# One block's second layer moved to the end part of a three-stage transformer kernel, with its activations parked in DRAM

## The chip, the core and the metric

The kernel runs on one core of one Trainium2 chip. The metric is the device time of one launch in microseconds (us), lower is better. The engines are named as the profile names them: PE (TensorE matmuls), PEld (weight loads), DVE (VectorE), ACT (ScalarE), POOL (GpSimd), SP (the queue from which most DMAs are issued).

## What is computed

Three stages follow each other: a masked attention, a gated layer pair with an RMS norm ahead of it, and a second layer pair with a leaky activation.

```python
# 4 batches, 8 heads, 576 positions, head size 64; heads 0-3 a window of 32, heads 4-7 every 4th of 128
scores = np.where(masks, scale * q @ k.T, -1e9)
x = softmax(scores) @ v                      # -> (2304, 512)
xn = x / sqrt(mean(x * x) + 1e-6) * rms_g
y = (silu(xn @ w_gate) * (xn @ w_val)) @ w_out      # 512 -> 1536 -> 512
h = y @ w_in                                        # 512 -> 2048
out = (max(h, 0) + alpha * min(h, 0)) @ w_out2      # 2048 -> 512
```

Inputs and the output are float32. The kernel splits each operand into two float16 halves (high and low) and adds three products (high by high, high by low, low by high) for each matrix product.

## The kernel before

The 2304 tokens are seven blocks: blocks 0, 1 and 5 have 256 tokens, blocks 2, 3, 4 and 6 have 384. In this text "A j" is the first layer pair of block j (`mm1`, `mm2`), 12 steps c of 128 hidden columns, and "B j" is the second one (`mm3`, `mm4`), 16 steps. In step c of B j, `mm3` makes 12 matmuls (4 slices of the model width by 3 half products) that stream the block's tokens, ACT and DVE form the activation (lines 984 and 985), ACT and POOL split it into halves, and two steps later `mm4` adds it into the block's sum with 3 matmuls of 512 columns for each 128 tokens. `y_out` (lines 957 to 966 of before) ends A j: it scales the 128-token tiles of y, splits them into halves in a tile `yhl`, and transposes them by a DMA from SP into `xy[j % 3]`, one of three buffers that hold a block's x and later its y.

The order of the phases is written out by hand: A0, A1, A2, B0, B1, B2, A3, then the first four steps of A4, B3, the rest of A4, A5, A6. Blocks 4, 5 and 6 have no B phase. Their second layer runs in an end part over pairs of 128-token tiles (list `tiles`, four pairs): `mm3_t` makes the same products as `mm3`, two steps c at a time, and `mm4_t` makes the last product in a form with 7 block products in place of 8, each a 128x256 product in three half products. So a pair needs 192 matmuls of 256 columns in `mm3_t` and 8 x 21 = 168 of 256 columns in `mm4_t`; the pair's sums are put together in `out_t` (m1o at line 1120, yo at lines 1123 to 1127). The weights of the end part's last product are made up in `remake`, during A6.

The attention runs beside the layers. It is cut into 156 steps, and `take` hands out steps in each slot (one slot is one step c of a phase): it looks at the x of which block is due when, and paces the steps evenly to that, with a planner's clock that counts 1.95 for 128 tokens in an A slot and 1.3 in a B slot. In A2 the credit is multiplied by `PACE`, 0.7. Most of the attention is in groups of up to 128 queries: a split into halves (ACT lines 539 to 542, DVE 548 to 553), a DMA transpose `qkT<-qkhl` (line 563, one for each group), scores, exponentials (line 589), a second DMA transpose `pT<-phl`, the product with v, and for half of the groups the norm. The tiles `qkhl` and `qkT` have one buffer each.

The weights are loaded, unpacked on DVE (lines 231 to 233) and split on ACT, DVE and POOL (lines 404 to 409) beside the first phases: those of the first pair in A0, those of the second one at the end of A2 and in B0. All decoded weights together fill 68 of 70 slots of the tile `wb`; slots of the first pair's weights come free as A6 uses them for the last time.

A tile scheduler with a timeline of its own sets the order of the instructions on each engine within the priorities that the code gives; attention steps have a higher priority.

Of the kernel before, what the change touches and what calls it, by code (L numbers as in the profile page):

```python
# [29 lines left out]
def kernel(  # L30
# [14 lines left out]
    nc = tc.nc  # L45
# [901 lines left out]
    def y_out(j):  # L947
# [6 lines left out]
        for n in range(nt):  # L954
            y = wk.tile([128, 2, DM], F16, tag="hl2", bufs=2, name="yhl")
            hl.append(y)
            nc.scalar.activation(y.rearrange("p a d -> p (a d)").bitcast(F32), acc[n], ACTF.Square, accum_out=ss[:, n:n + 1])
            nc.vector.tensor_scalar(ss[:, n:n + 1], ss[:, n:n + 1], 2.0 ** -100, None, ALU.max)
            rcn = rc[:, n:n + 1]
            if j >= NTJ:  # L960
                i = tiles.index((j, n))
                rcn = rct[:, i:i + 1]
            root_scale(ss[:, n:n + 1], sg[:, n:n + 1], rcn, 2.0 ** -62)
            nc.scalar.activation(y[:, 0, :], acc[n], ACTF.Copy, scale=sg[:, n:n + 1])
            nc.vector.scalar_tensor_tensor(y[:, 1, :], acc[n], sg[:, n:n + 1], y[:, 0, :], ALU.mult, ALU.subtract)
# [52 lines left out]

    NTJ = 4
    NP = C2 // 2  # L1020

    tiles = [(4, 0), (4, 1), (5, 0), (5, 1), (4, 2), (6, 2), (6, 0), (6, 1)]
    assert sorted(tiles) == [(j, n) for j in range(NTJ, NJ) for n in range(ncols(j) // 128)]
    NT = len(tiles) // 2
# [30 lines left out]
    def weight(cp, m, l):  # L1055
# [3 lines left out]
        return ts[cp][l][:, w]  # L1059

    def mm3_t(t, cp):
        tl = tail["tl"]
        ps = tail["ps3"].tile([128, 2, 256], F32, tag="p3", name="p3")
        (j0, n0), (j1, n1) = tiles[2 * t:2 * t + 2]
        if (j0, n0 + 1) == (j1, n1):
            parts = [(0, 256, xy[j0 % NXY][:, :, :, n0 * 128:n0 * 128 + 256])]
# [198 lines left out]
    for s in slots:  # L1265
        kind, j, c = s
        for f in take(dur(s) * (PACE if (kind, j) == ("A", 2) else 1.0)):
            f()
# [9 lines left out]
        if kind == "A" and j < 3:  # L1278
# [30 lines left out]
    for n in range(len(order) + 1):  # L1309
        if n < len(order):  # L1310
# [50 lines left out]
```

## Time and profile before

| | |
|---|---|
| median of 3 runs | 956.49 us (955.83 to 957.1) |
| the profiled execution's own time | 959.12 us |
| its span, first to last instruction | 956.9 us |
| busy: PE / DVE / ACT / POOL | 906.7 / 666.4 / 548.2 / 321.2 us |
| A2 ends and B0 begins (first activation of line 984) | 294.3 us |
| first output of B0, B1, B2 (line 1002) | 346.4, 391.1, 454.9 us |
| end of A3 (line 957) | 529.6 us |
| end of A5, and first matmul of the end part | 724.6 and 790.3 us |

The profiled execution is one run; its time is 2.6 us above the median of the three timed ones. A span is counted from the first to the last instruction. A busy PE means that matmuls were under way, not that they follow each other at the highest rate.

### The profile page before, as it was taken

What the parts mean: (1) busy time and instruction counts of PE and PEld (TensorE: products, weight loads), DVE (VectorE), ACT (ScalarE), POOL (GpSimd) and SP (SyncE); (2) the same over time, 40 slices, a digit from 0 to 9 for tenths busy, and PEclk for the clock granted to TensorE, in tenths of its full rate; (3) what the DMA queues carried; (4) which work ended last, traced back from release to release, by engine and by line L of the source; (5) the groups of instructions that cost most, each with busy time, mean ns of one, the idle gap of its engine ahead of it and who ended that gap; (6) DMA issues with size and microseconds to landing.
All of it is one profiled execution on the core that took longest, in us unless ns stands there. A gap on an engine that the chain in (4) does not pass through costs nothing.

```text
span 956.9 us, 18827 instructions
## 1 busy us (share of the span) xinstructions
PE 906.7 (95%) x6760; PEld 619.6 (65%) x6760; DVE 666.4 (70%) x1602; ACT 548.2 (57%) x1537; POOL 321.2 (34%) x324
## 2 busy tenths in 40 slices
PE   6568899999998999999999999999999999999997
PEld 4556676775556666555555555555775558889986
DVE  4999997998787766665766775334545837777674
ACT  3436587766799886766756776444534324344342
POOL 2222441131354544423332233333252622322221
PEclk9778999999999999999999999999999999999998
DMA  9992346545324555544554654232301001000000
GB/s 255 315 357 89 120 131 188 143 146 149 81 51 99 106 101 94 106 85 95 117 93 82 114 97 71 59 76 42 54 15 23 1 1 35 1 24 23 2 24 23
DMA packets 191613, 88.14 MB, mean 92 GB/s; under 512 B 176800, under 2 KB 180384, under 8 KB 191520
## 3 DMA queue, kind: packets, MB, share of 16 engines
q1 hardware_dynamic: 189504, 83.27, 37.9%
q10 hardware_dynamic: 2016, 3.67, 1.2%
q8 instruction: 53, 0.87, 0.4%
q14 instruction: 40, 0.33, 0.1%
HBM read 55.32 MB, written 6.55 MB: 65 GB/s over the span
## 4 chain that ended last, share of the span: by engine, by line
PE 74%; DVE 10%; DMA 6%; ACT 4%; issue 2%; SPq 2%; POOL 1%; DVEq 0%; ACTq 0%; POOLq 0%
PE psw L97 34%; PE acc L97 22%; PE p L97 16%; DMA wb<-in_moe_w_out_dram 2%; DVE wb L232 2%; DVE wb L233 2%; ACT wb L404 2%; DVE wb L231 1%; DVE wb L409 1%; SPq L212 1%; SPq L629 1%; DMA wb<-in_moe_w_val_dram 1%; DMA wb<-in_moe_w_gate_dram 1%; DMA wb<-in_q_dram 1%; PE psw L639 1%
## 5 line engine op out<-in xcount | busy, mean ns | idle before, releaser
L97 PEld LDWEIGHTS <-wb 128*128 128x128 f16 (+1 forms) x4866 | 452.3, 98 | 196.5 <-DVE wb L233 18.9
L97 PE MATMUL psw<-xyall,wb 128*128 128x384 f16 (+1 forms) x2784 | 425.0, 303 | 2.1 <-DVE sqo L284 1.2
L97 PE MATMUL acc<-wb,hlall 128*128 128x512 f16 x822 | 197.1, 379 | 1.9 <-ACT hlall L924 1.1
L97 PEld LDWEIGHTS <-hlall 128*128 128x128 f16 x822 | 79.1, 98 | 82.1 <-POOL hlall L930 1.4
L930 POOL TENSOR_TENSOR hlall<-t,hlall 128x384 f16<-128x384 f32 (+1 forms) x58 | 59.3, 1022 | 159.6 <-ACT hlall L924 140.0
L97 PE MATMUL acc<-wb 128*128 128x512 f16 (+1 forms) x402 | 83.1, 353 | 16.1 <-DVE wb L233 15.9
L97 PE MATMUL p<-xyall,wb 128*128 128x256 f16 (+1 forms) x960 | 88.7, 251 | 0.0
L1095 POOL TENSOR_TENSOR wb<-fa,wb 128x640 f16<-128x640 f32 x32 | 45.4, 1420 | 111.4 <-ACT wb L1094 111.4
L97 PE MATMUL p<-wb 128*128 128x256 f16 x672 | 77.6, 273 | 0.0
L921 DVE SCALAR_TENSOR_TENSOR t<-t,psw 128x384 f32<-128x384 f32 (+1 forms) x84 | 41.0, 488 | 47.0 <-ACT t L920 47.0
L920 ACT ACTIVATE t<-psw,tsc 128x384 f32<-128x384 f32 (+1 forms) x84 | 44.0, 524 | 50.1 <-PE psw L97 50.1
L589 ACT ACTIVATE s<-s,mx 96x128 f32<-96x128 f32 (+2 forms) x132 | 50.1, 381 | 23.4 <-DVE mx L581 21.1
L930 POOL TENSOR_TENSOR hlall<-p,hlall 128x256 f16<-128x256 f32 (+1 forms) x49 | 39.2, 801 | 51.6 <-ACT hlall L987 44.4
L404 ACT ACTIVATE wb<-wb,wsg 128x512 f16<-128x512 f32 x68 | 46.2, 711 | 17.1 <-DVE wsg L341 10.2
L1093 DVE SCALAR_TENSOR_TENSOR wb<-fa,wb 128x384 f16<-128x384 f32 x32 | 40.5, 1269 | 22.2 <-ACT wb L1092 22.1
L1094 ACT ACTIVATE wb<-fa 128x640 f16<-128x640 f32 x32 | 23.5, 735 | 55.6 <-DVE fa L1087 55.6
L705 POOL TENSOR_TENSOR phl<-s,phl 96x512 f16<-96x512 f32 (+2 forms) x33 | 36.4, 1104 | 54.2 <-ACT phl L699 37.3
L407 POOL TENSOR_TENSOR wb<-wb 128x512 f16<-128x512 f32 x28 | 37.5, 1345 | 42.1 <-ACT wb L406 22.6
L985 DVE SCALAR_TENSOR_TENSOR p<-m,oma,psw 128x256 f32<-128x256 f32 (+1 forms) x64 | 34.5, 540 | 24.4 <-ACT m L984 24.0
L930 POOL TENSOR_TENSOR wb<-t,wb 128x256 f16<-128x256 f32 (+1 forms) x26 | 27.2, 1046 | 69.7 <-ACT wb L924 69.7
L233 DVE SCALAR_TENSOR_TENSOR wb<-wb 128x512 int32<-128x512 int32 (+1 forms) x56 | 49.7, 891 | 0.3
L922 DVE SCALAR_TENSOR_TENSOR t<-t,psw 128x384 f32<-128x384 f32 (+1 forms) x84 | 41.1, 489 | 12.1 <-PE psw L97 11.0
(202 smaller groups left out, 1342.1 us busy)
## 6 DMA issues: line engine op xcount, KB each, us to landing
wb<-in_moe_w_out_dram SPq DMA_DIRECT2D x28, 512.0 KB, 4.5
wb<-in_moe_w_in_dram SPq DMA_DIRECT2D x16, 512.0 KB, 3.9
wb<-in_moe_w_gate_dram SPq DMA_DIRECT2D x12, 512.0 KB, 7.4
wb<-in_moe_w_val_dram SPq DMA_DIRECT2D x12, 512.0 KB, 7.3
out_dram<-o ACTq DMA_DIRECT2D x14, 256.0 KB, 3.2
rkv<-in_k_dram SPq DMA_DIRECT2D x23, 128.0 KB, 2.4
rkv<-in_v_dram SPq DMA_DIRECT2D x23, 128.0 KB, 2.7
rq<-in_q_dram SPq DMA_DIRECT2D x23, 96.0 KB, 2.2
```

The source lines that it names most:

```text
L97: nc.tensor.matmul(o, a, b, start=start, stop=stop)
L233: nc.vector.scalar_tensor_tensor(w, r[:, :, :, 0], 29, w, ALU.logical_shift_right, ALU.bitwise_or)
L404: nc.scalar.activation(half(b, 0), dec(b), ACTF.Copy, scale=wsg[:, s:s + 1])
L407: nc.gpsimd.tensor_tensor(half(b, 1), dec(b), half(b, 0), ALU.subtract)
L589: nc.scalar.activation(s[:nq, h, :nk], s[:nq, h, :nk], ACTF.Exp, bias=mx[:nq, 1, h:h + 1], scale=-1.0, accum_out=g["dn"][:nq, h])
L705: nc.gpsimd.tensor_tensor(phl[:nq, 1, :, :nk], g["s"][:nq, :, :nk], phl[:nq, 0, :, :nk], ALU.subtract)
L920: nc.scalar.activation(t[:, :T], pg[:, :T], ACTF.Tanh, scale=tsc[:, chunk(c):chunk(c) + 1])
L921: nc.vector.scalar_tensor_tensor(t[:, :T], t[:, :T], 1.0, pg[:, :T], ALU.add, ALU.mult)
L922: nc.vector.scalar_tensor_tensor(t[:, :T], t[:, :T], 2.0 ** -46, pv[:, :T], ALU.mult, ALU.mult)
L930: nc.gpsimd.tensor_tensor(a[:, 1, :T], t[:, :T], a[:, 0, :T], ALU.subtract)
L1093: nc.vector.scalar_tensor_tensor(l[:, 0:3], f[:, 0:3], 0.25, h[:, 0:3], ALU.mult, ALU.subtract)
L1095: nc.gpsimd.tensor_tensor(l[:, 3:8], f[:, 3:8], h[:, 3:8], ALU.subtract)
```

## The change

Block 0 loses its B phase. `EARLY = (1,2,3)` names the blocks that keep one. `y_out(0)` writes its two tiles of halves to DRAM (`ydram`) in place of transposing them into `xy[0]`, and marks block 0 as done, so that x of block 3 may go to `xy[0]`. The list `tiles` gets block 0's pair at its head, and the end part has five pairs. `fetch` takes two free slots of `wb` in A6 and transposes the halves from DRAM into them; `mm3_t` reads them from there. The phases are A0, A1, A2, B1, B2, A3, the first four steps of A4, B3, the rest of A4, A5, A6. What was tied to B0 (the rest of the weight loads, the splits of the second pair's weights) is tied to B1. The pace of the attention is 0.5 in A2 and 0.7 in B1.

```diff
+    EARLY = (1,2,3)
...
-            if j >= NTJ:
+            if j not in EARLY:
                 i = tiles.index((j, n))
                 rcn = rct[:, i:i + 1]
...
+            if (j, n) in y_at:
+                nc.sync.dma_start(out=ydram[y_at[j, n]], in_=y.rearrange("p a d -> p (a d)"))
+                continue
             nc.sync.dma_start_transpose(
...
+        if kept(j):
+            done_b.add(j)
...
-    tiles = [(4, 0), (4, 1), (5, 0), (5, 1), (4, 2), (6, 2), (6, 0), (6, 1)]
+    def kept(j):
+        return j not in EARLY and j + NXY < NJ
+
+    tiles = [(j, n) for j in range(NJ) if kept(j) for n in range(ncols(j) // 128)]
+    y_at = {jn: i for i, jn in enumerate(tiles)}
+    ydram = [dram.tile([128, 2 * DM], F16, name=f"ydram{i}") for i in y_at]
+    tiles += [(4, 0), (4, 1), (5, 0), (5, 1), (4, 2), (6, 2), (6, 0), (6, 1)]
...
+    def fetch(t):
+        if t >= NT or tiles[2 * t] not in y_at or t in y_in:
+            return
+        y_in[t] = pair()
+        to = wb16[:, y_in[t] * 1024:(y_in[t] + 2) * 1024].rearrange("p (a t) -> p a t", a=2 * KD)
+        for n in range(2):
+            nc.sync.dma_start_transpose(out=to[:, :, n * 128:(n + 1) * 128], in_=ydram[2 * t + n])
...
-        if (j0, n0 + 1) == (j1, n1):
+        if t in y_in:
+            i0 = y_in[t]
+            parts = [(0, 256, wb16[:, i0 * 1024:(i0 + 2) * 1024].rearrange("p (a k t) -> p a k t", a=2, k=KD))]
+        elif (j0, n0 + 1) == (j1, n1):
...
-    phases = [(p, j) for p in "AB" for j in range(3)]
-    for j in range(3, NTJ):
-        phases += [("A", j), ("B", j)]
-    phases += [("A", j) for j in range(NTJ, NJ)]
+    phases = [("A", j) for j in range(3)] + [("B", j) for j in range(3) if j in EARLY]
+    for j in range(3, NJ):
+        phases += [("A", j)] + [("B", j)] * (j in EARLY)
...
-        for f in take(dur(s) * (PACE if (kind, j) == ("A", 2) else 1.0)):
+        for f in take(dur(s) * (0.5 if (kind, j) == ("A", 2) else 0.7 if (kind, j) == ("B", EARLY[0]) else 1.0)):
...
-        if (kind, j) == ("B", 0):
+        if (kind, j) == ("B", EARLY[0]):
...
+        if (kind, j) == ("A", NJ - 1) and c and can_load():
+            fetch(0)
```

Line numbers of the change are one higher than before up to `y_out`, and 6 higher in `mm3`. Three places show how instructions move.

On SP, where `y_out(0)` stands (yhl are the halves of y, xd is an attention result on its way to DRAM), before:

```order
92 L610 DMA scratch<-xd 96x256
93 L966 DMA_TRANSPOSE xyall<-yhl 128x8x128 x2
94 L629 DMA wb<-in_q_dram 96x4x64
95 L629 DMA wb<-in_k_dram 128x4x64
96 L629 DMA wb<-in_v_dram 128x4x64
97 L610 DMA scratch<-xd 96x256
```

and with the change, there and at the end of SP's list, where the two tiles come back:

```order
92 L611 DMA scratch<-xd 96x256
93 L968 DMA ydram(0, 0)_104<-yhl 128x1024
94 L968 DMA ydram(0, 1)_105<-yhl 128x1024
95 L630 DMA wb<-in_q_dram 96x4x64
...
342 L758 DMA_TRANSPOSE xyall<-xhl 128x8x64
343 L1081 DMA_TRANSPOSE wb<-ydram(0, 0)_104 128x8x128
344 L1081 DMA_TRANSPOSE wb<-ydram(0, 1)_105 128x8x128
345 L970 DMA_TRANSPOSE xyall<-yhl 128x8x128 x5
346 L1013 DMA out_dram<-o 128x512 x3
347 L1013 DMA out_dram<-o 64x512 x4
```

Two transposes became two plain writes at the same place, and two transposes more stand after the attention's last and ahead of those of blocks 5 and 6.

On ACT, at the end of A2, from the last activation of the first layer (t<-psw) to the last split of its hidden values (hlall<-t); wb<-wb are weight splits, junk, qkhl, vhl and s are attention. Before:

```order
264 L920 ACTIVATE t<-psw,tsc 128x384
265 L513 ACTIVATE junk,ams<-rq 96x256
266 L406 ACTIVATE wb<-wb,wsg 128x512
267 L513 ACTIVATE junk,ams<-rkv 128x256
268 L404 ACTIVATE wb<-wb,wsg 128x512
269 L589 ACTIVATE s,dn<-s,mx 96x128 x4
270 L513 ACTIVATE junk,ams<-rkv 128x256
271 L924 ACTIVATE hlall<-t 128x384
```

and with the change:

```order
253 L921 ACTIVATE t<-psw,tsc 128x384
254 L605 ACTIVATE xd<-psw 96x256
255 L514 ACTIVATE junk,ams<-rq 32x256
256 L405 ACTIVATE wb<-wb,wsg 128x512 x2
257 L540 ACTIVATE qkhl<-rq,sc 32x4x2x64
258 L542 ACTIVATE qkhl<-rkv,sc 96x4x64
259 L543 ACTIVATE vhl_87<-rkv,sc 96x4x64
260 L514 ACTIVATE junk,ams<-rkv 96x256
261 L925 ACTIVATE hlall<-t 128x384
```

The four exponentials of a group no longer stand between the two; the next group's split does.

On ACT in A3, from its third activation to its fourth, before:

```order
538 L920 ACTIVATE t<-psw,tsc 128x384
539 L740 ACTIVATE xhl<-x 96x512
540 L589 ACTIVATE s,dn<-s,mx 96x128 x4
541 L924 ACTIVATE hlall<-t 128x384
542 L699 ACTIVATE phl<-s 96x512
543 L920 ACTIVATE t<-psw,tsc 128x384
```

and with the change:

```order
480 L921 ACTIVATE t<-psw,tsc 128x384
481 L700 ACTIVATE phl<-s 96x512
482 L605 ACTIVATE xd<-psw 32x256
483 L514 ACTIVATE junk,ams<-rq 96x256
484 L514 ACTIVATE junk,ams<-rkv 128x256
485 L925 ACTIVATE hlall<-t 128x384
486 L514 ACTIVATE junk,ams<-rkv 128x256
487 L540 ACTIVATE qkhl<-rq,sc 96x4x2x64
488 L542 ACTIVATE qkhl<-rkv,sc 128x4x64
489 L543 ACTIVATE vhl_86<-rkv,sc 128x4x64
490 L590 ACTIVATE s,dn<-s,mx 96x128 x4
491 L921 ACTIVATE t<-psw,tsc 128x384
```

More attention stands in this phase. From the first to the twelfth activation of A3 ACT has 77 rows before and 99 with the change. On DVE, from the first instruction of a phase to the first of the next, A2 has 144 instructions before and 134 with the change, B0 107 before and B1, which now follows A2, 109, B2 111 and 131, and A3 118 and 159.

## Rows read from the trace of the kernel before

**Rows 1.** The page: span, busy time, and busy tenths with TensorE's clock.

```profile
span 956.9 us, 18827 instructions
PE 906.7 (95%) x6760; PEld 619.6 (65%) x6760; DVE 666.4 (70%) x1602; ACT 548.2 (57%) x1537; POOL 321.2 (34%) x324
...
PE   6568899999998999999999999999999999999997
...
PEclk9778999999999999999999999999999999999998
```

**Rows 2.** Stretches: length, then busy PE, PEld, DVE, ACT, POOL, clock, DMA.

```profile
216.00:240.00 24.00, 24.00 (x141) 13.48 (x139) 20.46 (x50) 15.98 (x45) 4.42 (x5) 1.00 0.55 138
240.00:264.00 24.00, 22.09 (x132) 12.18 (x131) 18.15 (x50) 17.20 (x46) 8.20 (x8) 1.00 0.39 81
264.00:290.00 26.00, 26.00 (x168) 15.08 (x166) 21.16 (x44) 24.97 (x59) 12.87 (x12) 1.00 0.34 68
290.00:310.00 20.00, 17.23 (x145) 12.07 (x143) 15.66 (x50) 18.28 (x57) 8.96 (x9) 1.00 0.42 84
310.00:346.00 36.00, 35.44 (x272) 23.61 (x269) 25.94 (x70) 30.27 (x98) 18.64 (x24) 1.00 0.52 99
346.00:391.00 45.00, 45.00 (x334) 30.15 (x333) 29.82 (x72) 32.75 (x107) 19.61 (x26) 1.00 0.54 94
391.00:457.00 66.00, 66.00 (x428) 36.49 (x427) 42.47 (x111) 45.46 (x146) 20.36 (x21) 1.00 0.51 102
457.00:530.00 73.00, 73.00 (x474) 42.44 (x473) 47.05 (x117) 45.84 (x140) 25.38 (x26) 1.00 0.45 91
555.00:600.00 45.00, 45.00 (x285) 24.50 (x284) 28.42 (x77) 31.84 (x103) 17.19 (x19) 1.00 0.54 89
820.00:840.00 20.00, 20.00 (x186) 17.92 (x184) 15.84 (x35) 7.08 (x14) 6.22 (x5) 1.00 0.01 2
840.00:860.00 20.00, 20.00 (x185) 17.93 (x184) 14.61 (x34) 8.59 (x15) 5.67 (x4) 1.00 0.08 27
```

**Rows 3.** Who PE waited for, 216 to 360 us.

```profile
PE psw L97 <- DVE sg L340: 1.5, 1, 1.5
PE acc L97 <- ACT hlall L924: 1.1, 1, 1.1
PE psw L97 <- DVE t L921: 0.8, 1, 0.8
PE psw L97 <- DVE t L922: 0.7, 1, 0.7
PE acc L97 <- ACT hlall L987: 0.6, 1, 0.6
```

**Rows 4.** Chain that ended last, in B1: start, length, what.

```profile
349.65 1.31 PE psw L97 x12
350.96 1.29 PE acc L97 x6
```

**Rows 5.** The same chain in the end part, 815 to 845 us.

```profile
814.98 30.02 PE p L97 x275
```

**Rows 6.** Timeline of ACT: end of a tile pair in the end part.

```profile
837.84 0.38 ACT L1120 ACTIVATE m1o<-p 128x256 f32<-128x256 f32 x1
...
877.32 0.38 ACT L1120 ACTIVATE m1o<-p 128x256 f32<-128x256 f32 x1
```

**Rows 7.** DMA issues: KB each, median us to landing.

```profile
x<-scratch SPq DMA_DIRECT2D x12, 96.0 KB, 2.5
...
xyall<-yhl SPq DMA_TRANSPOSE x18, 3.2
...
al<-in_moe_alpha_dram SPq DMA_DIRECT2D x1, 8.0 KB, 9.7
```

**Rows 8.** Timeline of SP: transposes of y, blocks 0, then 5 and 6.

```profile
155.44 3.02 SPq L966 DMA_TRANSPOSE xyall<-yhl  x2
...
728.69 76.48 SPq L966 DMA_TRANSPOSE xyall<-yhl  x5
```

**Rows 9.** Timeline of PE: the end part's first matmuls.

```profile
790.28 0.93 PE L97 MATMUL p<-xyall,wb 128*128 128x256 f16 x7
```

**Rows 10.** Timeline of SP: one transpose for each attention group.

```profile
554.40 1.46 SPq L563 DMA_TRANSPOSE qkT<-qkhl  x1
563.64 1.59 SPq L563 DMA_TRANSPOSE qkT<-qkhl  x1
573.22 1.40 SPq L563 DMA_TRANSPOSE qkT<-qkhl  x1
```

**Rows 11.** The exponentials of the attention: ns min/median/max.

```profile
L589 ACT ACTIVATE s<-s,mx x132: 357/385/403, 257.9 to 684.5; 96x128 f32<-96x128 f32 x92, 32x96 f32<-32x96 f32 x24, 64x96 f32<-64x96 f32 x16
```

More of the change, by code (lines that the diff above doesn't have):

```diff
@@ L1009, in o_tile @@
             col += m
-    NTJ = 4
     NP = C2 // 2
-    tiles = [(4, 0), (4, 1), (5, 0), (5, 1), (4, 2), (6, 2), (6, 0), (6, 1)]
-    assert sorted(tiles) == [(j, n) for j in range(NTJ, NJ) for n in range(ncols(j) // 128)]
+    def kept(j):
[4 more added lines that the diff above has]
+    tiles += [(4, 0), (4, 1), (5, 0), (5, 1), (4, 2), (6, 2), (6, 0), (6, 1)]
+    assert sorted(tiles) == [(j, n) for j in range(NJ) if j not in EARLY for n in range(ncols(j) // 128)]
+    assert len(y_at) % 2 == 0
     NT = len(tiles) // 2
@@ L1059, in weight @@
         return ts[cp][l][:, w]
+    y_in = {}
+    def fetch(t):
[5 more added lines that the diff above has]
+            nc.sync.dma_start_transpose(out=to[:, :, n * 128:(n + 1) * 128], in_=ydram[2 * t + n])
     def mm3_t(t, cp):
@@ L1142 @@
     PACE = 0.7
-    phases = [(p, j) for p in "AB" for j in range(3)]
-    for j in range(3, NTJ):
-        phases += [("A", j), ("B", j)]
-    phases += [("A", j) for j in range(NTJ, NJ)]
-    ahead = {j + 1 for n, (p, j) in enumerate(phases) if p == "A" and phases[n + 1:n + 3] == [("B", j), ("A", j + 1)]}
+    phases = [("A", j) for j in range(3)] + [("B", j) for j in range(3) if j in EARLY]
+    for j in range(3, NJ):
+        phases += [("A", j)] + [("B", j)] * (j in EARLY)
+    ahead = {j + 1 for n, (p, j) in enumerate(phases) if p == "A" and j > 2 and phases[n + 1:n + 3] == [("B", j), ("A", j + 1)]}
     slots = []
@@ L1282 @@
             state["pump"] -= int(state["pump"])
-        while (kind, j, c) == ("B", 0, 0) and (made or loaded or later):
+        while (kind, j, c) == ("B", EARLY[0], 0) and (made or loaded or later):
             pump(1)
-        if (kind, j) == ("B", 0):
+        if (kind, j) == ("B", EARLY[0]):
             for b in range(NW1 + (2 * c + 2 if c else 0), min(NW1 + 2 * c + 4, NBLK)):
@@ L1315 @@
                 tail["a"] = deque((slot16(), slot16()) for _ in range(LAGT + 2))
+            if cp == 3 * (t > 0) + 2:
+                fetch(t + 1)
             mm3_t(t, cp)
+            if t in y_in and cp == NP - 1:
+                give(y_in[t], y_in[t] + 1)
             if units:
```

## The prediction

> **What bounds the kernel now.** I read the page first: PE is busy for 906.7 of 956.9 us, and the slices show where it is not, in the first eighth and a little around a third of the span; TensorE's granted clock is at nine tenths or more, the level of 2.4 GHz, from the fifth slice to the last but one [rows 1]. So a microsecond off PE's work is a microsecond off the time wherever PE is not waiting, and elsewhere the waits decide. The table of stretches says which is which [rows 2]: PE is busy without a gap in B1 (346 to 391), B2 (391 to 457), A3 (457 to 530) and in the end part (820 to 860), while DVE and ACT are busy for two thirds of the time. The stretch from the middle of A2 to the end of B0 has gaps: 24.00 - 22.09 = 1.91 us at 240 to 264, 2.77 at 290 to 310, 0.56 at 310 to 346, 5.2 us together. The list of waits of PE there names single events of 0.6 to 1.5 us [rows 3]: a PSUM tile that waits for a DVE queue (L340, L921, L922), or a hidden tile that waits for ACT (L924, L987). They come where weight splits, attention and the ends of A1 and A2 meet on DVE and ACT.
>
> **The change part by part.** *PE work of B0, removed.* `mm3` makes 16 x 12 = 192 matmuls of 256 columns, `mm4` 16 x 2 x 3 = 96 of 512. In B1, which has the same shape, a run of 12 of the first kind takes 1.31 us and one of 6 of the second 1.29 us [rows 4], 109.2 and 215 ns each. B0 is 192 x 0.1092 + 96 x 0.215 = 20.97 + 20.64 = 41.6 us.
>
> *PE work of the fifth tile pair, added.* 192 + 168 = 360 matmuls of 256 columns. In the end part 275 of them in a row take 30.02 us [rows 5], 109.2 ns each: 39.3 us. The other way to read it is the distance of two pair ends, 877.32 - 837.84 = 39.5 us [rows 6]. So the move gives 2.3 us, and 2.1 at least. It is the seven products in place of eight that give it: 96 matmuls of 512 columns, 192 units of 256, become 168 such units.
>
> The Trainium skill (TensorE: Matmul & The Clock Gate, section Back-to-back issue gap) speaks against this: it gives about 131 ns for a matmul of 512 columns and 81 ns for one of 128 in a sustained stream of weight loads and matmuls. By these figures 96 x 0.131 = 12.6 us would become at least 168 x 0.081 = 13.6 us, a loss of 1 us or more in place of the gain. The rows say 215 and 109 ns, so the sum goes by them; the page's other formula, N/2.4 + 2.5 ns, is the one that this trace agrees with.
>
> *The other engines in the end part.* A pair more is 8 more rounds of activation, sums and splits. In a full stretch of the end part DVE has 15.84 of 20 us, ACT 7.08, POOL 6.22, and PE 20.00 [rows 2], across a pair's end too (840 to 860). PE's own work covers them: 0. If DVE came to its limit, 20 - 15.84 = 4 us in 20 would be left before PE waits.
>
> *The way through DRAM.* At `y_out(0)` two transposes (3.02 us of SP's time [rows 8]) become two plain writes; nobody waits for them, and what stands behind them on SP moves up by a little. In A6 `fetch` issues two transposes from DRAM. The trace has no transpose from DRAM; the nearest are 3.2 us to landing for one from SBUF, and 2.5 to 9.7 us for plain reads from DRAM [rows 7]. I take 3.2. They wait for two slots that A6 gives back in its first steps, soon after 728.69, where SP issues the transposes of block 5 [rows 8]; the end part begins at 790.28 [rows 9]. Behind them on SP are the transposes of block 5, needed one pair later than before. Even at 9.7 us each some 30 us of A6 cover them: 0. Without that cover it would be 2 x 3.2 = 6.4 us.
>
> *The waits around A2.* B1 takes B0's place with the weight splits (109 DVE instructions by the order, B0 had 107), and the attention in A2 is paced lower: DVE has 134 instructions in A2 for 144 before. At the end of A2 the queue ahead of the split for which PE waited 1.1 us [rows 3] is as long as before: four exponentials, 4 x 0.385 = 1.5 us [rows 11], are gone, three instructions of the next group's split stand there. The waits at 240 to 264 belong to the unpacking of weights, which is unchanged. Bounds: all 5.2 us vanish, or as much again comes in, since B1 is laid out as B0 was. I take -0.5, a tenth of the waits, for a fourteenth less work on DVE.
>
> *The attention's new place.* No attention work is saved; B0's 41.6 us of PE time, under which it ran, are gone. Pacing puts it into B2 and A3: by the order DVE has 131 instructions for 111 in B2, and 159 for 118 in A3. With the mean of the stretch (42.47/111 and 47.05/117 us [rows 2]) DVE gets to 42.5 + 20 x 0.383 = 50 of 66 us in B2 (76%), and to 47.1 + 41 x 0.402 = 63.5 of 73 in A3 (87%). Nearest rows: 216 to 240 has DVE at 85% and 264 to 290 has ACT at 96%, both without a gap in PE; 310 to 346 with DVE at 72% and ACT at 84% has 0.56 in 36 us [rows 2]. In B2 and A3 7 and 8 groups are split, one for each 9.3 us; at that distance (9.24 and 9.58 us) they ran between 554 and 573 [rows 10] beside a PE without a gap [rows 2]. Bounds: 0, and 139 us at the rate of 290 to 310 (2.77 in 20), 19 us, which had phase ends and weight splits in it that B2 and A3 have not. I take 0.4, near the rows without a gap.
>
> *Sum.* -41.6 + 39.3 - 0.5 + 0.4 = -2.4 us: the profiled execution of 959.12 us (span 956.9 and 2.2 around it) becomes 956.7, and the median of 956.49, 2.6 us lower than that execution, becomes 954.1. A measurement of this kernel tells about 0.2%, 1.9 us, from no change.
>
> **The rivals.** *The new place eats the gain.* A3 and B2 wait at the rate of 310 to 346 (0.56/36): 139 us x 1.6% = 2.2 us more, and the time is 956.3. For it speaks DVE at 87% in A3, where the activation chain of the first layer (L920 to L922) stands in the same queues; against it the rows at equal load without a gap. Between 0.5 and 4 us of new waits, 954.7 to 958.4.
>
> *Slower.* The single buffers of qkhl and qkT make the attention late in A3, and PE, in whose list the scores and value products stand between the layers' matmuls, stops at each. At 0.5 us on each of the 15 groups of B2 and A3 this is 7.5 us, 954.1 - 0.4 + 7.5 = 961.2 us. It is slower from 2.4 + 1.9 = 4.3 us of new waits, 0.3 us for each group. For it: waits of 0.6 to 1.5 us are just what PE shows where queues are full [rows 3]. Against it: the 9.24 us above.
>
> *More gain.* With a group fewer in A2 and the B phase starting with fewer groups under way, 3 of the 5.2 us of waits go: 954.1 - 2.5 = 951.6. Against it: B1 is laid out as B0 was.
>
> *The move loses PE time.* It does if a matmul of 512 columns takes under 168 x 109.2 / 96 = 191 ns; at 180 ns, 96 x 0.011 = 1.1 us would be lost, and with the waits unchanged the time is 957.6. The 215 ns in B1 [rows 4] are clear of it. This is the case of the sustained figures in the Trainium skill's page named above.
>
> **How the numbers follow.** The forecast (waits between -1.5 and +0.5 in all, 952.7 to 954.7) has 0.44, the first rival 0.31, slower 0.12, more gain 0.12, the last 0.01. The time is that of the likeliest, 954.1. More gain reaches down to 949.0, where all 5.2 us of waits are gone, and slower begins at 958.4; a range from 950.8 to 958.6 leaves out about half of the one and nearly all of the other, 0.18. Faster by over 0.2% is below 954.6: 0.43 + 0.12 = 0.55. Within 0.2% is 0.33, slower 0.12.
>
> **What would show it.** In the profile of the changed kernel the end part is 39.3 to 39.5 us longer from its first p matmul to the end (now 166.6 us from 790.28), with PE busy throughout; it begins about 42 us earlier; acc matmuls number 96 fewer and p matmuls 360 more. PE has no gap over 0.5 us in B2 and A3 and about 4.5 us of gaps from A2 to B1. I am wrong if PE waits in A3 for L921, L922 or a qkT or pT transpose by more than 2 us in all, or if the first p matmuls wait for wb.

## The result: 967.0 us in place of 956.8, and where the profile shows it

The changed kernel takes 967.0 us (median of 4 runs, 965.92 to 969.14), the kernel before 956.8 beside it (955.83 to 957.79): a ratio of 1.0109, interval 1.0089 to 1.013. It is slower by 10.2 us; the forecast was 954.1, with a range from 950.8 to 958.6. The page of the changed kernel, against [rows 1]:

```profile
span 965.4 us, 19015 instructions
...
PE 908.5 (94%) x6832; PEld 627.8 (65%) x6832; DVE 687.1 (71%) x1646; ACT 550.7 (57%) x1530; POOL 322.8 (33%) x316
...
PE   6568899999999999889999999999999999999997
...
PEclk9778899999999999999999999999999999999999
```

PE has nearly the same work as before (908.5 us for 906.7), the granted clock is at the level of 2.4 GHz as before, and the span is 8.5 us longer, so PE waits more. (The spans differ by less than the medians because the profiled execution of the kernel before was 2.3 us above its median, that of the changed one 0.2; what follows accounts for the 8.5 us.) The slices (24.1 us each) say where: two eights stand now at 386 to 434 us, where the kernel before had nines.

**The end part** did as forecast. Timeline of PE at its start, of ACT at the pair ends, of SP where block 0's y comes back:

```profile
759.71 0.93 PE L98 MATMUL p<-wb 128*128 128x256 f16 x7
...
807.27 0.38 ACT L1145 ACTIVATE m1o<-p 128x256 f32<-128x256 f32 x1
846.57 0.38 ACT L1145 ACTIVATE m1o<-p 128x256 f32<-128x256 f32 x1
886.05 0.38 ACT L1145 ACTIVATE m1o<-p 128x256 f32<-128x256 f32 x1
...
695.14 1.23 SPq L1081 DMA_TRANSPOSE wb<-ydram(0, 0)_104  x1
696.47 1.26 SPq L1081 DMA_TRANSPOSE wb<-ydram(0, 1)_105  x1
```

The pair ends are 39.3 and 39.5 us apart; the part takes 965.4 - 759.71 = 205.7 us for 166.6 [rows 9], 39.1 more, and PE's list of waits is empty there. PE's acc matmuls are 96 fewer (1128 for 1224) and its p matmuls 360 more (1992 for 1632), as forecast. The two transposes of block 0's y are issued at 695 and 696 us, 63 us before the first p matmul, and land 3.4 and 3.7 us later. But the part begins 30.6 us earlier, not 42 (759.71 for 790.28): the other 11 us are lost ahead of it. The stretches of the changed kernel (columns as in [rows 2]):

```profile
240.00:264.00 24.00, 23.01 (x139) 12.80 (x137) 17.49 (x45) 18.29 (x50) 7.23 (x7) 1.00 0.38 80
...
290.00:310.00 20.00, 18.81 (x155) 13.16 (x153) 16.27 (x47) 18.32 (x58) 9.23 (x10) 1.00 0.46 95
310.00:346.00 36.00, 35.82 (x267) 22.89 (x265) 27.69 (x76) 32.65 (x104) 18.37 (x22) 1.00 0.48 97
346.00:391.00 45.00, 42.35 (x275) 23.51 (x274) 33.18 (x79) 33.21 (x109) 21.80 (x22) 1.00 0.62 123
391.00:430.00 39.00, 35.68 (x243) 19.94 (x241) 26.34 (x79) 29.24 (x96) 10.47 (x11) 1.00 0.60 118
430.00:460.00 30.00, 28.51 (x198) 16.78 (x197) 22.19 (x63) 22.63 (x75) 10.50 (x11) 1.00 0.68 133
460.00:500.00 40.00, 36.93 (x243) 20.99 (x241) 26.09 (x68) 26.47 (x85) 14.07 (x14) 1.00 0.44 88
```

From 346 to 500 (block 2's second layer, B2, and block 3's first, A3) PE stands 2.65 + 3.32 + 1.49 + 3.07 = 10.5 us, where the kernel before had no gap in these two stages [rows 2]. No engine is full there: DVE is busy for 0.74, 0.68, 0.74 and 0.65 of the stretches, ACT for 0.66 to 0.75. Whom PE waited for, from 345 to 500 us (us in all, times, longest):

```profile
PE psw L98 <- DMA qkT<-qkhl: 6.3, 5, 2.0
PE psw L98 <- DMA pT<-phl: 3.3, 3, 1.6
PE psw L98 <- DVE sc L530: 0.8, 1, 0.8
```

The attention's transposed tiles are late, and hardly anything else (0.8 of 10.4 us). In the median they land as soon as before within 0.1 us, as the view of the tile qkT shows for the kernel before (386 to 530 us, the first fence) and for the changed one (340 to 500, the second):

```profile
who waited for it (us, times):
  DVE s L572: 5.5, 4
...
DMA to landing us min/median/max: 3.4/3.8/5.2
```

```profile
L564 SPq DMA_TRANSPOSE qkT<-qkhl x15: 1292/1442/2630, 346.5 to 494.3; - x15
...
  PEld L98: 9.9, 7
  PE psw L98: 6.3, 5
...
DMA to landing us min/median/max: 3.3/3.9/5.7
```

The landing takes 3.9 us in the median for 3.8; what is gone is the time between landing and use. In the kernel before, PE's first use of a qkT tile came 1.9 to 10.8 us behind its landing, in each of the 12 groups. In the changed one it came at once, 0.04 us behind the landing, in 7 of 15 groups: there PE was waiting for the tile. (The view lists these 7 at the weight load, and 5 of them again at the matmul behind it.) Three of the 7 also took long to land, 4.5, 4.8 and 5.7 us. A piece of the chain that ended last shows two of them:

```profile
421.53 4.84 DMA qkT<-qkhl
...
426.46 0.46 ACT qkhl L540
...
427.09 0.49 ACT qkhl L542
...
428.38 5.68 DMA qkT<-qkhl
434.06 0.04 issue
434.11 0.65 PE psw L98 x8
```

One group's transpose lands, the next group's split starts at once, its transpose is issued 2 us later, lands 5.7 us later, and the score starts 0.05 us behind it.

For sums I count waits as the time from one matmul's start to the next's beyond its columns at 2.4 GHz, where that is over 0.12 us. A busy row swallows part of this: the 10.5 us above are 12.3 us so counted. The count also holds what matmuls lose where the granted clock is at 0.50, the level of 1.2 GHz. In B2 and A3 this happens in neither of the two kernels; in some of the runs below it does, in b_cut, m_old, m_noT, m_noTT and m_qkhl2 behind a wait of 1.8 to 2.7 us, and costs up to 1.7 us a stage (more in m_qk2e and m_ldq). The account, before and after:

| | A0, A1 | A2 | B0 | B1 | B2 | A3 | A4 to A6, B3 | end |
|---|---|---|---|---|---|---|---|---|
| before, us | 223.9 | 85.5 | 37.0 | 44.8 | 63.8 | 74.7 | 262.8 | 164.6 |
| after, us | 225.0 | 79.9 | - | 40.0 | 72.0 | 82.1 | 262.7 | 203.7 |
| waits before | 41.6 | 5.7 | 0.7 | 0 | 0 | 0 | 1.7 | 0 |
| waits after | 40.8 | 2.6 | - | 0.9 | 6.6 | 5.7 | 1.7 | 0 |

(A stage runs here from one first activation of y or of the output to the next, A2 to that of its third tile, and the end counts from the y of block 6.) From A2 to A3 305.7 us became 274.0: 9.4 us of waits came in, so 41.1 us of other time, the columns, are gone. With the end's 39.1 and 1.1 us more at the start, where other runs differ by as much either way, that is 8.5 us, the difference of the spans.

### The profile page after: what moved, and what is told of

It is laid out like the page before. It is cut to its first block, busy times and chain, and to the rows that moved or that the text cites. A ratio compares the mean times of both kernels' runs of the same rounds, so it can differ in the third digit from the quotient of the medians.

```text
span 965.4 us, 19015 instructions
## 1 busy us (share of the span) xinstructions
PE 908.5 (94%) x6832; PEld 627.8 (65%) x6832; DVE 687.1 (71%) x1646; ACT 550.7 (57%) x1530; POOL 322.8 (33%) x316
## 4 chain that ended last, share of the span: by engine, by line
PE 70%; DVE 11%; DMA 8%; ACT 5%; issue 3%; SPq 2%; POOL 1%; ACTq 0%; DVEq 0%; POOLq 0%
PE psw L98 31%; PE p L98 20%; PE acc L98 18%; DMA qkT<-qkhl 2%; DVE wb L233 2%; DVE wb L234 2%; DVE wb L232 1%; DVE wb L410 1%; DMA rkv<-in_k_dram 1%; DMA wb<-in_moe_w_out_dram 1%; ACT s L590 1%; ACT wb L405 1%; SPq L213 1%; SPq L630 1%; DMA pT<-phl 1%
## 5 line engine op out<-in xcount | busy, mean ns | idle before, releaser
L98 PEld LDWEIGHTS <-wb 128*128 128x128 f16 (+1 forms) x4950 | 462.2, 99 | 189.9 <-DVE wb L234 19.1
L98 PE MATMUL psw<-xyall,wb 128*128 128x384 f16 (+1 forms) x2592 | 402.8, 306 | 2.5 <-DVE sqo L285 1.2
L98 PE MATMUL p<-wb 128*128 128x256 f16 x1032 | 117.6, 273 | 0.0
L1120 POOL TENSOR_TENSOR wb<-fa,wb 128x640 f16<-128x640 f32 x40 | 56.7, 1419 | 139.5 <-ACT wb L1119 139.5
L98 PE MATMUL acc<-wb 128*128 128x512 f16 (+1 forms) x318 | 63.0, 347 | 16.4 <-DVE wb L234 16.3
L1118 DVE SCALAR_TENSOR_TENSOR wb<-fa,wb 128x384 f16<-128x384 f32 x40 | 50.7, 1270 | 28.3 <-ACT wb L1117 28.2
L921 ACT ACTIVATE t<-psw,tsc 128x384 f32<-128x384 f32 (+1 forms) x84 | 44.0, 524 | 42.7 <-PE psw L98 41.1
L1119 ACT ACTIVATE wb<-fa 128x640 f16<-128x640 f32 x40 | 29.4, 735 | 67.5 <-DVE fa L1112 67.5
L405 ACT ACTIVATE wb<-wb,wsg 128x512 f16<-128x512 f32 x68 | 46.2, 711 | 18.8 <-DVE wsg L342 10.2
L931 POOL TENSOR_TENSOR hlall<-p,hlall 128x384 f16<-128x384 f32 (+1 forms) x43 | 36.8, 859 | 45.3 <-ACT hlall L993 38.1
L925 ACT ACTIVATE hlall<-t 128x384 f16<-128x384 f32 (+1 forms) x59 | 28.3, 479 | 40.9 <-DVE t L923 40.8
L923 DVE SCALAR_TENSOR_TENSOR t<-t,psw 128x384 f32<-128x384 f32 (+1 forms) x84 | 41.0, 488 | 11.3 <-PE psw L98 10.4
L1105 ACT ACTIVATE mi<-p 128x512 f32<-128x512 f32 x40 | 23.7, 593 | 43.2 <-PE p L98 43.2
```

Of the source, the lines that this page charges most:

```text
L98: nc.tensor.matmul(o, a, b, start=start, stop=stop)
L405: nc.scalar.activation(half(b, 0), dec(b), ACTF.Copy, scale=wsg[:, s:s + 1])
L921: nc.scalar.activation(t[:, :T], pg[:, :T], ACTF.Tanh, scale=tsc[:, chunk(c):chunk(c) + 1])
L923: nc.vector.scalar_tensor_tensor(t[:, :T], t[:, :T], 2.0 ** -46, pv[:, :T], ALU.mult, ALU.mult)
L931: nc.gpsimd.tensor_tensor(a[:, 1, :T], t[:, :T], a[:, 0, :T], ALU.subtract)
L1118: nc.vector.scalar_tensor_tensor(l[:, 0:3], f[:, 0:3], 0.25, h[:, 0:3], ALU.mult, ALU.subtract)
```

## Experiments

The theory after the result is **cover**: B0's 41.6 us were time in which the attention's chain (loads, squares, split, transpose, scores, exponentials, transpose, values) ran beside PE. The first block's work at the end of the program can't give this, because blocks 3 and 4 need the attention before their first layers. So its steps, two to a group besides the norms, are asked for in less time, faster than the chain can follow, and PE stands at the tile that is not there yet. Rivals: the new paces alone, the single buffer of qkT, the load of DVE and ACT, the place of the steps in PE's order, the way through DRAM. By the planner's rule the steps taken in A2, B0, B1, B2, A3 are 11, 9, 9, 13, 15 before and 10, -, 8, 19, 20 after. All results in one table (ratio to the kernel before on the same chip, with its 95% interval; waits in us, as above, those of m_pad's added work under B0+B1):

| | us | ratio | steps B2, A3 | waits A2 | B0+B1 | B2 | A3 |
|---|---|---|---|---|---|---|---|
| before | 956.8 | | 13, 15 | 5.7 | 0.7 | 0 | 0 |
| after | 967.0 | 1.0109 [1.0089, 1.013] | 19, 20 | 2.6 | 0.9 | 6.6 | 5.7 |
| b_pace | 958.98 | 1.0012 [1.0001, 1.0023] | 15, 17 | 5.6 | 0.2 | 2.0 | 0 |
| m_old | 964.66 | 1.0065 [1.004, 1.009] | 15, 18 | 8.2 | 2.7 | 3.9 | 1.2 |
| m_even | 963.04 | 1.0052 [1.0039, 1.0066] | 14, 16 | 8.7 | 4.3 | 1.0 | 0 |
| m_front | 971.35 | 1.0137 [1.0117, 1.0157] | 13, 14 | 18.9 | 5.3 | 0 | 0 |
| m_noT | 968.56 | 1.0109 [1.0078, 1.014] | 19, 20 | 6.1 | 1.3 | 4.8 | 5.8 |
| m_qk2e | 972.99 | 1.0152 [1.0127, 1.0176] | 19, 20 | 3.2 | 0.9 | 9.0 | 7.7 |
| m_ldq | 997.24 | 1.0404 [1.0381, 1.0427] | 19, 20 | 6.5 | 0.9 | 19.3 | 10.5 |
| b_cut | 929.06 | 0.9687 [0.9656, 0.9718] | 19, 20 | 2.5 | 0.9 | 7.6 | 4.5 |
| m_pad | 1003.02 | 1.0456 [1.0426, 1.0486] | 15, 17 | 2.7 | 3.1 | 3.9 | 1.2 |
| b_dve | 974.96 | 1.0179 [1.0137, 1.022] | 13, 15 | 4.1 | 1.1 | 0 | 0 |
| b_dve2 | 960.4 | 1.0023 [1.0005, 1.004] | 13, 15 | 5.6 | 0.7 | 1.8 | 0 |
| m_off | 967.39 | 1.0083 [1.0066, 1.0101] | 19, 20 | 3.9 | 0 | 7.0 | 4.8 |
| m_noTT | 960.82 | 1.0028 [1.0015, 1.0041] | 19, 20 | 3.5 | 0.9 | 2.6 | 3.7 |
| m_noL | 965.68 | 1.007 [1.0047, 1.0092] | 19, 20 | 6.0 | 0 | 5.6 | 2.7 |
| m_noLT | 957.45 | 0.9996 [0.9981, 1.001] | 19, 20 | 5.1 | 0.9 | 1.8 | 0 |
| m_qkhl2 | 966.19 | 1.0078 [1.006, 1.0096] | 19, 20 | 2.8 | 0.9 | 4.3 | 6.6 |
| m_lda | 974.01 | 1.0167 [1.0147, 1.0187] | 19, 20 | 4.1 | 0.2 | 5.8 | 3.9 |
| me_lda | 965.89 | 1.0079 [1.006, 1.0098] | 14, 16 | 7.1 | 0.5 | 1.8 | 0 |

The kernel before took 958.0 to 958.6 us beside the experiments and 956.8 beside the change; the ratios allow for it.

**Paces.** b_pace is the kernel before with the change's paces alone; m_old, m_even and m_front are the change with other factors:

```
-        for f in take(dur(s) * (0.5 if (kind, j) == ("A", 2) else 0.7 if (kind, j) == ("B", EARLY[0]) else 1.0)):
+        for f in take(dur(s) * (0.7 if (kind, j) == ("A", 2) else 1.0 if (kind, j) == ("B", EARLY[0]) else 1.0)):
```

(m_old; m_even has 1.0 and 1.0, m_front 1.2 and 1.2, b_pace 0.5 and 0.7 with B0 for B1.)

> The kernel before with the paces of the change (0.5 in A2, 0.7 in B0) and nothing else: B2 gets 15 attention steps for 13, A3 17 for 15. Theory A (PE waits where groups follow each other faster than the chain of transposes and scores): +1 to +4 us, with gaps at scores (qkT) in B2 or A3. Theory B (the missing 41.6 us of B0 is the cause, wherever the steps stand): no change, 956 to 958 us.

> The change with the paces of before (0.7 in A2, 1.0 in B1): A2 13 steps for 10, B1 11 for 8, B2 15 for 19, A3 18 for 20. Theory A: part of the 13 us of gaps in B2 and A3 goes, 958 to 962 us. Theory B: the gaps move to A2 and B1, 964 to 968 us.

> The change with pace 1.0 in A2 and B1: A2 17 steps for 10, B1 10 for 8, B2 14 for 19, A3 16 for 20, near what the kernel before has in B2 and A3 (13, 15). Theory A: B2 and A3 are almost without gaps, 955 to 959 us. Theory B: 964 to 968 us, gaps in A2.

> The change with pace 1.2 in A2 and B1: A2 20 steps, B1 10, B2 13, A3 14, fewer than before in A3. Theory A: no gaps in B2 and A3; A2 has twice the steps that it had and may wait there, 954 to 960 us. Theory B: 964 to 968 us.

The paces alone cost 0.1%: they are not the cause. B2 waits a little in that run (2.0 us), as theory A has it, and the time is 0.75 us over the kernel before, a little less than theory A's 1. With the change, m_old is in the range of theory B; m_even (963.0) is between the ranges, and m_front (971.4) over both. In the change the paces move the waits to wherever the steps are dense and don't take them away: 15.8 us from A2 to A3 with the change's own, 16.0, 14.0 and 24.2 with the others. Among the kernels of the table that differ in paces alone, and m_pad and b_cut below, the order is one: B2 (64 us) has no wait at 13 steps, 1 to 4 us at 14 or 15, 6.6 and 7.6 at 19; A3 (75 us) none at 14 to 16, 0 to 1.2 at 17 or 18, 4.5 to 5.7 at 20. So in these two stages waits begin near 4.5 us a step.

**Single suspects.** m_noT feeds the scores and values from weights that stay in SBUF, so that PE waits for neither transposed tile (the attention's values are wrong by that):

```
-        qT, kT = g["qT"], g["kT"]
+        d = hl_at[b_g(0)]
+        qT = wb16[:, d * 1024:(d + 1) * 1024].rearrange("p (a t) -> p a t", t=128)
+        kT = half(b_v(0), 0).rearrange("p (a t) -> p a t", t=128)
...
-        pT, v_ = g["pT"], vhl[g["vi"]]
+        d = hl_at[b_g(1)]
+        pT = wb16[:, d * 1024:(d + 1) * 1024].rearrange("p (a t) -> p a t", t=128)
```

> The change, with the scores and the value products of the transposed groups fed from resident weights in place of qkT and pT (so the attention's numbers are not those of the reference); both transposes still run, unread. Theory L (PE stands because transposed tiles land late): the waits on qkT and pT, 12 us in B2 and A3, go: 953 to 957 us. Theory E (DVE and ACT are too full there): other waits take their place, 962 to 967 us. Theory Q (SP's queue is too full): as L.

The time stays (968.6 us, a little over the range of theory E), and PE waits for other tiles: for work on DVE (L926, L995, in the layers' activations) and ACT (L514, the squares of a group's inputs). m_qk2e gives every other group a second qkT in two free weight slots and issues the transpose right behind the split:

> The change with a second buffer for qkT (in the two slots of wb that are free from the end of B1 to the start of A4), used by every other group, and the transpose issued right after the group's split, half a step pair earlier. Theory L, with the single buffer as the cause of the lateness: the qkT waits of B2 and A3 (8.3 us) go, pT's 3.7 stay, 957 to 961 us. Theory E and Q: 964 to 968 us.

It is no better (973.0 us, over both ranges): the longest waits are now for pT (5.3 us). m_off places the steps 100 instead of 400 priorities ahead (`OFF = 100`):

> The changed kernel with the attention's steps placed 100 instead of 400 priorities ahead of the feed-forward's instructions, so that their matmuls stand less far ahead in TensorE's order. Theory 'cover' (the steps are asked for faster than a group's chain can go): the waits stay or move, 962 to 972. Theory 'placed too far ahead' (TensorE stands at a score that it could have taken a few matmuls later): the waits in block 2's second and block 3's first layer fall by more than half, 955 to 960.

The waits stay (11.8 us in B2 and A3 for 12.3) and the time is in the range of theory *cover*: the place of the steps in PE's order, as far as this moves it, is not the cause.

**The load.** b_dve puts unread DVE work into B2 and A3 of the kernel before; the scheduler, which sees no dependence, set it at the program's start (A0 166.7 us for 151.4; B2 and A3 have DVE's work of before), so the run says nothing on its question. b_dve2 ties the same work to the evictions:

```
         a = hl_take(j, c)
+        for _ in range(4 if j == 3 else 0):
+            nc.vector.tensor_scalar(dj, t[:, 0:256], 0.5, None, ALU.mult)
...
+        for _ in range(2 if j == 2 else 0):
+            nc.vector.tensor_scalar(dj, p[:, 0:256], 0.5, None, ALU.mult)
```

> The kernel before with extra work on DVE that nobody reads: 32 scalings of 256 columns in B2 and 48 in A3, about 0.3 us each, 10 and 15 us, so that DVE is as full as in the changed kernel. Theory E: gaps in PE in B2 and A3, 962 to 968 us. Theories L and Q: 956 to 959 us.

> The kernel before with more VectorE work that nobody needs, tied to the evictions of block 3's first layer (four multiplications of 256 columns behind each) and of block 2's second (two behind each), so that they run there and nowhere else. The profile of the changed kernel has VectorE and ScalarE at some 0.72 busy where TensorE waits. Theory 'load' (a share of busy time like that is enough to make the attention late): TensorE waits there now too, 962 to 968. Theory 'chain' (what counts is how many of the attention's groups are asked for in a time, not the load): 956 to 960.

Its stretches, B2 and A3:

```profile
392.00:457.00 65.00, 63.66 (x412) 34.85 (x410) 49.32 (x141) 43.58 (x139) 20.45 (x21) 1.00 0.46 97
457.00:532.00 75.00, 75.00 (x485) 43.55 (x484) 63.81 (x166) 47.40 (x145) 26.90 (x26) 1.00 0.49 94
```

DVE is at 0.76 and 0.85, above the changed kernel's 0.65 to 0.74, and A3 has no gap; the time, 960.4 us, is at the upper edge of theory *chain*. The load of DVE is not it. The 1.8 us of waits in B2 are for hidden tiles behind the added work. ACT was not loaded here (0.67 and 0.63); m_noLT below has it at 0.81 and 0.76 almost without a gap.

**Cover.** b_cut is the kernel before with B0 left out (block 0's rows of the output are not written) and the change's paces, with no way through DRAM and four pairs at the end (its core):

```
-    phases = [(p, j) for p in "AB" for j in range(3)]
+    phases = [("A", j) for j in range(3)] + [("B", j) for j in (1, 2)]
```

m_pad is the change with PE work of B0's size between A2 and B1, on weights that are there, its result unused (its core):

```
+    phases = [("A", j) for j in range(3)] + [("P", 0)] + [("B", j) for j in range(3) if j in EARLY]
...
+        for n in range(12):
+            mm(ps[:, 0:256], half(b_g(c % C1), 0)[:, 0:128], half(b_v(c % C1), 0)[:, 0:256], n == 0, n == 11)
+        for n in range(6):
+            mm(ps2, half(b_g(c % C1), 0)[:, 0:128], half(b_v(c % C1), 0), n == 0, n == 5)
```

> The kernel before with block 0's second layer left out altogether (its rows of the output are not written), and the paces of the change (0.5 and 0.7) around block 1's; no y goes through DRAM and the end part keeps four pairs. Block 0's second layer was 41.6 us of TensorE time, so a kernel that loses just these columns takes 956.5 - 41.6 = 915. Theory 'cover' (those 41.6 us were time in which the attention's other engines caught up): the same waits as in the changed kernel, some 10 to 13 us more of them between the third block's first layer and the fourth's, 925 to 929. Theory 'way through DRAM or fifth pair' (the changed kernel's loss comes from what was added): 914 to 918.

> The changed kernel with 16 slots of TensorE work between block 2's first layer and block 1's second that nobody needs: in each 12 matmuls of 256 columns and 6 of 512 on weights that lie in SBUF, and two reads of one column by VectorE, so as many columns as block 0's second layer had there (41.6 us), and nothing of its transfers or evictions. Its results are not used. Theory 'cover': the waits in block 2's second and block 3's first layer vanish (they were about 12 us), and the time is 967 + 41.6 - 12 = 995 to 999. If the loss is not one of cover: 967 + 41.6 = 1007 to 1010.

b_cut, B2 and A3, and PE's waits there:

```profile
345.00:417.00 72.00, 66.66 (x430) 36.78 (x428) 49.97 (x132) 52.63 (x174) 29.71 (x30) 0.98 0.57 114
417.00:498.00 81.00, 77.02 (x516) 44.25 (x514) 56.03 (x153) 57.69 (x186) 27.32 (x28) 1.00 0.56 116
```

```profile
PE psw L97 <- DMA pT<-phl: 3.7, 3, 1.8
PE psw L97 <- DVE sc L529: 2.6, 1, 2.6
PE psw L97 <- DMA qkT<-qkhl: 1.4, 1, 1.4
PE psw L97 <- DVE sc L530: 1.4, 1, 1.4
```

With nothing moved and nothing added nearly the same idle time of PE is there, 9.3 us for 10.5 (5.34 + 3.98; 12.1 as starts count, 1.4 of it at the lower clock). The kernel is 929.06 - (958.61 - 41.6) = 12.0 us over what its columns ask (9.7 by the spans, 925.0 and 956.9), at the upper edge of the range of *cover*. The tiles that come last are again links of the attention's chain, though not in the same shares: 5.1 us are for transposed tiles and 4.0 for the split's scales `sc` on DVE. So taking B0 away is enough for the loss; neither the way through DRAM nor the fifth pair is needed for it. m_pad tries the other direction:

```profile
389.00:459.00 70.00, 67.94 (x439) 38.04 (x437) 45.87 (x118) 47.12 (x151) 23.66 (x25) 1.00 0.45 99
459.00:536.00 77.00, 77.00 (x494) 44.42 (x493) 54.21 (x134) 52.26 (x164) 26.00 (x27) 0.98 0.45 103
```

The idle time is 2.06 us for 10.5, the waits 5.1 for 12.3; the 1.2 of these in A3, where the row shows no gap, are matmuls at a granted clock of 0.50 (459.0 to 461.7 us, behind a group's short matmuls with a wait of 0.8 us). Its time is 1003.0, between the two ranges: the planner gave the pad 9 steps but left 15 and 17 in B2 and A3, where waits begin, and from A2 to B1 5.9 us of waits stand for 3.5. By 967.0 x 958.61 / 956.8 + 41.0 (the pad's columns) = 1009.8 without cover, it gives back 6.8 us. So PE time between A2 and B1 takes most of the waits out of B2 and A3, and a little over half of the 12 us out of the time.

**What can't go faster.** m_noTT leaves the attention's transposes out altogether, m_noL the loads of groups 26 to 42 (they compute on one pair of tiles filled with 0.5), m_noLT both (all three compute wrong values by that). The transposes are those of queries, keys and weights, from group 19 on, and PE reads resident weights in their place as in m_noT. m_qkhl2 is the change with a second buffer for the split. The core of the first and of the second:

```
-        nc.sync.dma_start_transpose(out=qkT[:, :, :nk], in_=g["qk"][:nk])
...
-        nc.sync.dma_start_transpose(out=g["pT"][:, :, :nq], in_=phl[:nq].rearrange("p a h c -> p (a h c)"))
```

```
+        if 26 <= i < 43:
...
+            g["rq"], g["rkv"] = kept_q
+            return
```

> The changed kernel with scores and values fed from resident weights (as in the run before without that wait), and the attention's transposes of queries, keys and weights now left out altogether, from group 19 on (numbers not the reference's). So nothing of the loop split, transpose, next split is left, and SP's queue has only loads and y's transposes. Theory 'transposes' loop' (the one split buffer, busy from the split's first write until the transpose has read it): the waits of block 2's second and block 3's first layer fall from 12.3 us to under 4, and the time to 955 to 961. Theory 'engines' chain' or 'loads': as before, 964 to 970.

> The changed kernel with the loads of queries, keys and values of groups 26 to 42 (those of block 2's second and block 3's first layer) left out: these groups all compute on one pair of tiles filled once with 0.5 (numbers not the reference's). Theory 'loads' (they wait on SP's queue for their buffers, ahead of transposes): the waits there fall from 12.3 us to under 4, 955 to 961. Theory 'transposes' loop' or 'engines' chain': a part of it at most, 962 to 968.

> Both: no transposes of the attention from group 19 on, and no loads for groups 26 to 42 (numbers not the reference's). What still waits is the chain on ScalarE, VectorE and GpSimd. Theory 'engines' chain': still over 6 us of waits in block 2's second and block 3's first layer, 962 to 968. The other two: under 3 us, 954 to 959.

> The changed kernel with a second buffer for the split queries and keys, in two free weight slots, used by every other group between the end of block 1's second layer and block 4's first. Theory 'transposes' loop': this takes the loop apart, the waits there fall by more than half, 957 to 962. If that loop does not bind: 965 to 970.

m_noLT from 345 to 499 us (its A3 ends at 489, and up to there the shares are the same within 0.01):

```profile
345.00:417.00 72.00, 70.51 (x470) 39.88 (x467) 54.91 (x145) 58.19 (x194) 30.36 (x31) 1.00 0.11 28
417.00:499.00 82.00, 82.00 (x567) 48.73 (x566) 62.92 (x180) 62.15 (x199) 28.39 (x29) 1.00 0.16 41
```

With the same steps and DVE and ACT busier than in the changed kernel (DVE 0.76 and 0.77, ACT 0.81 and 0.76), PE stands 1.5 us, and the time is that of the kernel before, in the range given for loads and transposes. So the engines can take 39 steps there; what can't keep up is what goes through SP's queue, the loads and the transposes. Each holds a part: 6.3 of 12.3 us are left without the transposes (1.7 of the 6.3 at the lower clock), 8.3 without the loads, 1.8 without both. The time without transposes, 960.8, is at the edge of the range given, but under 4 us of waits were expected; without loads, 965.7 is in the range of 'a part of it at most'. m_qkhl2 (10.9 left) says that the one split buffer alone doesn't bind either. Two buffers at once, for qkT and the split, and more buffers for the loads were not tried.

SP is not short of time to issue. In the changed kernel from 340 to 500 us it stands for 83 us in all, waiting for other engines. The longest entry is loads whose buffer the split has to give back first, and the kernel before has it too (386 to 530 us, the second line):

```profile
SPq L502 <- DVE qkhl L549: 20.7, 11, 6.3
```

```profile
SPq L501 <- DVE qkhl L548: 16.0, 8, 5.6
```

**Another queue.** m_ldq issues the loads from GpSimd, m_lda from ScalarE, me_lda too with the paces 1.0 and 1.0 (`nc.gpsimd.dma_start` or `nc.scalar.dma_start` for `nc.sync.dma_start` in `a_load`).

> The change with the attention's loads of q, k and v issued from POOL's queue in place of SP's, so that transposes do not stand behind them. Theory Q: the waits on qkT and pT halve or go, 955 to 961 us. Theories L and E: 965 to 970 us.

> The changed kernel with the attention's loads of queries, keys and values issued by ScalarE in place of SP; SP's queue keeps the transposes and the rest. Theory 'one queue' (a load that waits for its buffer holds up the transposes behind it): as with the loads left out or a little over it, waits of block 2's second and block 3's first layer down from 12.3 us to about 8, 964 to 966. Theory 'transfer times': 966 to 969, or more if ScalarE now stands at the buffers' waits, as GpSimd did when the loads were its own.

> The same with the paces 1.0 and 1.0, the fastest pair so far (963.0 with the loads on SP). Theory 'one queue': 959 to 962, still not under the kernel before, whose B0 hides more. Theory 'transfer times' or ScalarE standing: 963 or more.

In m_ldq GpSimd then stands itself at the buffers, 340 to 500 us:

```profile
POOL rq L502 <- DVE qkhl L549: 24.3, 12, 4.8
POOL rq L502 <- DVE dn L600: 12.1, 1, 12.1
```

and the kernel is 29 us slower than the change beside the same kernel before, over all the ranges given; that these waits are the whole of it is not shown. On ScalarE (974.0 us, over the range given for theory *transfer times*) the waits of B2 and A3 fall from 12.3 to 9.7 us; but A0 and A1 take 4.9 us more than in the change, and A4 to A6 with B3 3.8. With even paces they are 1.8 us, but 1.0 with the loads on SP (m_even), and the time is 965.9 for 963.0. Neither is under the change with the same paces. Whether it is the order in SP's queue, the buffers or the sum of load, split and transpose times within a group that sets the 4.5 us a step stays open. No version here beats the kernel before: m_even at 1.0052 is the fastest that computes everything with B0 moved.

## Why the prediction was wrong, step by step

- *PE work of B0, removed* (41.6): right. From A2 to A3 the time outside waits fell by 41.1 us.
- *PE work of the fifth pair, added* (39.3 to 39.5): right, 39.1. The Trainium skill's sustained figures (TensorE: Matmul & The Clock Gate, section Back-to-back issue gap), by which the move would have lost time, don't hold here: the pair ends are 39.3 to 39.6 us apart, 109 ns for each of 360 matmuls of 256 columns, and one of 512 took 215 ns [rows 4].
- *The other engines in the end part* and *the way through DRAM* (0): right, PE waits for neither.
- *The waits around A2* (-0.5): mis-sized. From A2 to B1 6.4 us of waits became 3.5, so the term is -2.9 (the gaps of [rows 2] there, 5.2 us, became 0.99 + 1.19 + 0.18 = 2.4 in the same stretches). The paces did this, and not the layout of B1: with the old paces (m_old) 10.9 us stand there. It was paid for behind it, since the steps that the paces took out of these stages went to B2 and A3.
- *The attention's new place* (+0.4): **this step failed.** It measured 12.3 us. I set the cost by the busy shares of DVE and ACT and took the rows without a gap as the nearest. The load itself was no heavier than forecast: DVE was busy for 51.7 us in B2 and 56.8 in A3, where I had 50 and 63.5. But the share does not set the wait: DVE at 0.85 (b_dve2, A3) stands beside a PE without a gap, and at 0.65 to 0.74 beside one that waits. What counts is how fast the steps are asked for, against what the loads and transposes of a group can follow. The change asks for 39 steps in the 138.5 us that B2 and A3 had, one each 3.6 us; the kernel before had 28 there, one each 4.9 us, and waits begin near 4.5.
- The argument that I set against *Slower*, two distances of 9.24 and 9.58 us between groups beside a PE without a gap [rows 10], had left out the transpose ahead of these rows, issued 7.04 us before the one at 554.40. Its tile landed at 550.86 us and was used at 550.90, with nothing to spare, and just ahead of it, at 547.1, stands the only wait of PE that the list names between 360 and 800 us, for a tile pT (the chain that ended last and PE's list of waits, both of the kernel before):

```profile
543.56 3.53 DMA pT<-phl
547.36 3.50 DMA qkT<-qkhl
550.90 4.96 PE psw L97 x40
```

```profile
PE psw L97 <- DMA pT<-phl: 0.4, 1, 0.4
```

So where groups stood densest, the kernel before had no time left between landing and use. The stretch around [rows 10] (B3 and A4) asks for 26 steps in 143 us, one each 5.5 us, and is no measure for 3.6. In the changed kernel two groups come as close as 6.85 us (421.53 and 428.38, above).
- The rival *Slower* had the place, the stage and the tiles right (PE stops at qkT and pT in B2 and A3, over 2 us in all, which I had named as what would prove me wrong), with 7.5 us. Its mechanism, single buffers, is not shown: one buffer more for qkT or for the split, each by itself, does not help.

In sum: -41.1 + 39.1 - 2.9 + 12.3, and 1.1 us at the start, make the 8.5 us of the spans. That taking B0's time away is the cause (*cover*) is shown by b_cut and, for a little over half of the loss, by m_pad; that loads and transposes together are what can't follow, by m_noLT; which part of them, and why, is not shown.

## What to carry to other kernels

Before moving work of a saturated engine, ask who uses its time. PE's B0 did two jobs: its own columns, and 41.6 us in which the attention's chain came up to date. Moving it gained 2.0 us in columns and brought 9.4 us more waits. Price such a chain by the rate at which its steps are asked for, against the densest rate at which the trace shows them kept over a whole stage, and not by busy shares; and look for the densest place of the trace first, since the time left there between landing and use says how near the limit is. A change that takes a stage out can be tried by leaving the stage out: b_cut alone, which needs no moved code, would have shown the loss.

## What the runs showed that was not expected

The attention's transposes take nearly the same time to land in the kernel where they hold PE up (3.9 us in the median for 3.8); before, the 1.9 to 10.8 us between landing and use hid them. Loads moved to GpSimd's queue made the kernel 29 us slower and on ScalarE's 6 us, with the same bytes; GpSimd stood 36.4 us between 340 and 500 us at the buffers that its loads wait for. And taking away PE's wait for the tiles alone (m_noT, 968.6 us) gave nothing, while taking away the transposes themselves as well (m_noTT, 960.8 us) gave 7.7 us.
